# Interleaving feed-forward and attention in finer parts, and moving unused matmuls within the head

## The chip, the cores and the metric

The kernel runs on one core of a Trainium2 chip. The metric is the device time of one execution in microseconds (us). The profile's span, from the first to the last instruction, is about 1.8 us shorter than that time, and I use spans and parts of spans where I compare traces. Engines: PE is TensorE (matmuls), PEld its weight loads, DVE is VectorE, ACT is ScalarE, POOL is GpSimd, SP is SyncE, which issues DMAs. Matmuls write to PSUM; "evacuation" is ACT or DVE copying a finished PSUM tile to SBUF.

Each execution also has a mean granted clock of TensorE, as a share of full speed.

## The reference

Sinkhorn attention, then a bilinear feed-forward. There are 4 batches, 8 heads, 768 tokens and head size 64; tokens form 8 blocks of 96.

```python
for _ in range(5):                       # sort_net: [4, 8, 8, 8]
    P = exp(P - max(P)); P /= sum(P, -1); P /= sum(P, -2)
k_sorted = einsum('bhij,bhjcd->bhicd', P, k_blocks)      # "mix" of k
v_sorted = einsum('bhij,bhjcd->bhicd', P, v_blocks)      # "mix" of v
attn = softmax(scale * q_block @ k_sorted_block.T)       # 96 x 96 in each block
x = attn @ v_sorted                      # -> [3072, 512]
out = (x @ w_a) * (x @ w_b) @ w_out      # 512 -> 1536 -> 512
```

## The kernel before

All matmuls are bf16. PE's order is fixed by hand: in each stretch the feed-forward of one batch is the stream, and the attention of the next batch is cut into units that are placed between its steps. The first batch is split in two halves. The head (0 to 22 us) is the softmax iterations and the first half batch's attention, with nothing to interleave, so the author added unused matmuls (`keep_busy`).

```python
def keep_busy(ps, n, cols=512):          # unused matmuls on zeros
    for _ in range(n):
        nc.tensor.matmul(ps[:, 0:cols], lhsT=warm[:, 0:P], rhs=warm[:, 0:cols], ...)
...
keep_busy(heat[:, 0], (0, 4, 3, 2, 4)[it])          # in softmax iteration `it`
...
half_mix(0, 0, "k", "act", fill=2, cols=256)        # fill: keep_busy ahead of the mix
half_mix(0, 2, "k", "act", fill=1)
half_mix(0, 3, "k", "act", fill=1)
half_mix(0, 3, "v", "act", fill=1)
```

The attention of one head pair g, as units of the full stretches. The unit `o` multiplies the exponentials of the scores by v; a transpose of its result (the "x turn") then feeds the feed-forward. The array is used in three shapes: mixes and q turns as two column halves (128x64), scores as two row halves (64x128), and everything else whole (128x128, or 96 rows of it).

```python
def c_(g):                               # one unit
    if g < 2 * HP: turn_q(g)             # transposes of q, 128x64
    stage_mix(g, "k", ("act",))          # 12 matmuls, 128x64
    stage_mix(g, "v", ("dve", "act"))    # 12 matmuls, 128x64
    ...
def s_(g):                               # one unit
    stage_scores(g)                      # two halves of 8 matmuls, 64x128
    if g < 2 * HP: turn_v(g)             # transposes of v, whole array
def o_(g):                               # one unit
    stage_o(g)                           # two halves of 8 matmuls, whole array
    to_xT(g); ...
for n in range(HP + 1):
    if n < HP: us += [c_(g0 + n), s_(g0 + n)]       # (as closures)
    if n > 0:  us += [o_(g0 + n - 1)]
```

The feed-forward steps between which units go: `ffn_ab` makes one 128x384 tile of both first products (4 + 4 matmuls of 384 columns, tiles `pf`), `ffn_out` one block of the second product (12 matmuls of 512 columns, tile `po`). In the second half of batch 0, five first products were started early.

The softmax here doesn't subtract the row's maximum and nothing guards it: scores larger than these inputs give would overflow.

Of the kernel before, what the change touches and what calls it, by code (L numbers as in the profile page):

```python
# [9 lines left out]
FP32 = mybir.dt.float32  # L10
BF16 = mybir.dt.bfloat16
AF = mybir.ActivationFunctionType
# [10 lines left out]
def kernel(  # L23
# [11 lines left out]
    nc = tc.nc  # L35
    P = 128
    B, H, S, D = q.shape
    NB = sort_net.shape[-1]
# [126 lines left out]
    def keep_busy(ps, n, cols=512):  # L165
        for _ in range(n):
            nc.tensor.matmul(ps[:, 0:cols], lhsT=warm[:, 0:P], rhs=warm[:, 0:cols],  # L167
                             start=True, stop=True)
# [134 lines left out]
            nc.sync.dma_start_transpose(out=vss[g % NBUF][:, :, V0:V0 + P],  # L303
                                        in_=to.rearrange("p i t -> p (i t)"))

    def stage_scores(g):
        kT, qT, eT = kTs[g % NBUF], st[g, "qT"], eTs[g % NBUF]
        for hf in range(2):
            sc = psA.tile([P, 2, 512], FP32, tag="A", name="sc")
            for i in range(NBH):  # L310
                for e in range(2):
                    blk = hf * NBH + i
                    nc.tensor.matmul(  # L313
                        sc[:, e, i * BLK:(i + 1) * BLK],
                        lhsT=kT[e * D:(e + 1) * D, blk * BLK:blk * BLK + P],
                        rhs=qT[e * D:(e + 1) * D, :, blk * CG:(blk + 1) * CG],
                        start=True, stop=True)
            nc.scalar.activation(out=eT[:, hf, :, 0:HB], in_=sc[0:BLK, :, 0:HB],  # L318
                                 func=AF.Exp, scale=float(scale))

    def stage_o(g):
        xp = att.tile([BLK, NB, 2, D], BF16, tag="xp", name="xp")
        for hf in range(2):
            one_o(eTs[g % NBUF], hf, vss[g % NBUF], hf * NBH, xp, NB)
        st[g, "xp"] = xp

    def to_xT(g):
        xT, xp = xT_of(g // HP), st[g, "xp"]
# [17 lines left out]
    def hT_of(b):  # L346
        if b not in hTs:
            hTs[b] = ffp.tile([P, KO, S], BF16, tag="hT", name="hT")
        return hTs[b]

    def ffn_ab(b, m, t, begun=()):
        hT = hT_of(b)
        ab = []
        for n, w_sb in enumerate((w_a_sb, w_b_sb)):
            if n < len(begun):
                pf, k0 = begun[n], KA - 1
            else:
                pf, k0 = psF.tile([P, 512], FP32, tag="F", name="pf"), 0
            ab_mms(pf, w_sb, b, m, t, range(k0, KA))
            ab.append(pf)  # L360
            if n == 0:
                a_sb = ffp.tile([P, HW], BF16, tag="a_sb", name="a_sb", bufs=4)
                nc.scalar.copy(out=a_sb, in_=pf[:, 0:HW])  # L363
        nc.vector.tensor_mul(out=hT[:, m, t * HW:(t + 1) * HW], in0=a_sb,  # L364
                             in1=ab[1][:, 0:HW])

    def ffn_last(b, c):
        hT = hTs[b]
# [9 lines left out]

    def ffn_out(b, c):
        if b == B - 1 and c == NCH - 1:  # L380
            ffn_last(b, c)
            return
        hT = hTs[b]
        po = psF.tile([P, DMODEL], FP32, tag="F", name="po")
        for m in range(KO):
            nc.tensor.matmul(po, lhsT=hT[:, m, c * P:(c + 1) * P], rhs=w_out_sb[:, m, :],  # L386
                             start=(m == 0), stop=(m == KO - 1))
        o_sb = ffp.tile([P, DMODEL], FP32, tag="o_sb", name="o_sb", bufs=3)
        copy("act" if c % 2 == 0 else "dve", o_sb, po)
        if b == 0:  # L390
            h, u = divmod(c, 3)
            for c2 in range(2):
                nc.sync.dma_start(
                    out=_ap(out, (h * PH * NCH + 2 * u + c2) * DMODEL,
                            [[NCH * DMODEL, PH], [1, DMODEL]]),
                    in_=o_sb[c2 * PH:(c2 + 1) * PH])
        else:
            rows = out[b * S:(b + 1) * S, :].rearrange("(p c) n -> c p n", c=NCH)
            nc.sync.dma_start(out=rows[c], in_=o_sb)


    with tc.manual_schedule(engines={ET.PE, ET.Pool, ET.SP}):
        with tc.manual_schedule(engines={ET.Activation, ET.DVE}):
# [7 lines left out]
            for it in range(5):  # L411
# [14 lines left out]
                if it > 0:  # L426
                    nc.tensor.matmul(heat[0:NB, 1, 0:NB], lhsT=rsum, rhs=rsum,
                                     start=True, stop=True)
                    keep_busy(heat[:, 0], (0, 4, 3, 2, 4)[it])
                nc.vector.tensor_mul(out=p_nat, in0=p_nat,  # L430
                                     in1=_ap(rsum, 0, [[NB, BH], [1, NB], [0, NB]]))
                nc.vector.reduce_sum(out=csum, in_=p_nat.transpose([0, 2, 1]), axis=AX.X)
# [29 lines left out]
            load_ab(2)  # L462
            load_ab(3)

            half_mix(0, 0, "k", "act", fill=2, cols=256)
            half_mix(0, 0, "v", "dve")
            to_columns(1)
            half_mix(0, 1, "k", "act")
# [2 lines left out]
            half_scores(0, 0)  # L471
            half_v(0, 0)
            half_mix(0, 1, "v", "dve")
            half_mix(0, 2, "k", "act", fill=1)
            half_o(0, 0)
            half_scores(0, 1)
            half_v(0, 1)
            half_mix(0, 2, "v", "act")
            half_mix(0, 3, "k", "act", fill=1)
            half_x(0, 0, "dve")  # L480
            half_o(0, 1)
            half_scores(0, 2)
            half_v(0, 2)
            half_mix(0, 3, "v", "act", fill=1)
            half_x(0, 1, "dve")
            half_o(0, 2)
            half_scores(0, 3)
# [27 lines left out]


        def units_half():
            Q = [lambda hp=hp: half_q(1, hp, "dve") for hp in range(HP)]

            def M(hp):  # L520
                half_mix(1, hp, "k", "act")
                half_mix(1, hp, "v", "act")

            def R(hp):
                half_scores(1, hp)
                half_v(1, hp)

            us = [Q[0], lambda: M(0), Q[1]]
            for hp in range(HP):
                if hp + 1 < HP:  # L530
                    us.append(lambda hp=hp: M(hp + 1))
                us.append(lambda hp=hp: R(hp))
                if hp + 2 < HP:
                    us.append(Q[hp + 2])
                if hp > 0:
                    us.append(lambda hp=hp: half_x(1, hp - 1, "dve"))
                us.append(lambda hp=hp: half_o(1, hp))
            us.append(lambda: half_x(1, HP - 1, "dve"))
            return us

        def units_full(b):
            g0, us = b * HP, []

            def c_(g):
                if g < 2 * HP:
                    turn_q(g)
                stage_mix(g, "k", ("act",))
                stage_mix(g, "v", ("dve", "act"))
                if 2 * HP <= g < 3 * HP:
                    nc.gpsimd.tensor_copy(out=gate, in_=kTs[g % NBUF][0:1, 0:1])  # L550
                    load_pair(3, g % HP)

            def s_(g):
                stage_scores(g)
                if g < 2 * HP:
                    turn_v(g)

            def o_(g):
                stage_o(g)
                to_xT(g)  # L560
                if g < 2 * HP:
                    stage_q(g + HP)
                if 3 * HP <= g + 3 < B * HP:
                    pair_q(g + 3)
                    stage_q(g + 3)

            for n in range(HP + 1):
                if n < HP:
                    us.append(lambda g=g0 + n: c_(g))
                    us.append(lambda g=g0 + n: s_(g))  # L570
                if n > 0:
                    us.append(lambda g=g0 + n - 1: o_(g))
            return us

        def interleave(steps, units, spare, slow=0):
            n, done = len(steps), 0
            for s, step in enumerate(steps):
                step()
                want = s + 1 if s < slow else -(-(s + 1) * len(units) // (n - spare))
                while done < min(want, len(units)):  # L580
                    units[done]()
                    done += 1

        def paced(ab, po, units, spare):
            steps = [(1, f) for f in ab] + [(2, f) for f in po]
            total = sum(t for t, f in steps) - 2 * spare
            now = done = 0
            for t, step in steps:
                step()
                now += t  # L590
                while done < len(units) and done * total < now * len(units):
                    units[done]()
                    done += 1

        steps = [lambda: ffn_ab(0, 0, 0, begun[0:2]), lambda: ffn_ab(0, 1, 0, begun[2:4]),
                 lambda: ffn_ab(0, 2, 0, begun[4:5])]
        steps += [lambda m=m: ffn_ab(0, m, 0) for m in range(3, KO)]
        interleave(steps, units_half(), 1, 3)

        for b in range(B):  # L600
            ab = [lambda m=m, t=t, b=b: ffn_ab(b, m, t)
                  for m in range(KO) for t in range(2) if b > 0 or t == 1]
            po = [lambda c=c, b=b: ffn_out(b, c) for c in range(NCH)]
            paced(ab, po, units_full(b + 1) if b + 1 < B else [], 3 if b == 0 else 2)


# [28 lines left out]
```

## Time and profile before

| | before |
|---|---|
| time, median of 6 runs | 250.89 us (250.7 to 251.3) |
| span of the profile | 249.2 us |
| head, to the first feed-forward matmul | 21.70 us |
| second half of batch 0, to 48.45 | 26.75 us |
| batch 1's attention, to 90.06 | 41.61 us |
| batch 2's attention, to 144.59 | 54.53 us |
| batch 3's attention, to 199.11 | 54.52 us |
| feed-forward of batch 3 alone | 50.10 us |

From the page of the kernel before: the span, PE's busy time, the granted clock in 40 slices (in tenths), and the chain of waits by engine.

```profile
span 249.2 us, 5660 instructions
...
PE 239.0 (96%) x2330; PEld 139.8 (56%) x2342; DVE 112.8 (45%) x267; ACT 102.8 (41%) x203; POOL 59.4 (24%) x83
...
PEclk9999999999999999999999999999999999999999
...
PE 90%; DMA 2%; POOL 2%; DVE 2%; issue 1%; ACT 1%; POOLq 0%; DVEq 0%
```

PE bounds the kernel. But "96% busy" is no measure of headroom: a matmul's recorded duration overlaps the next one's (a `pf` matmul of 384 columns is recorded with 327 ns, and the next one starts 162 ns after it). So I read PE by the gap from one matmul's start to the next one's: 162 ns at 384 columns and 216 ns at 512, when nothing breaks the stream.

The timeline of PE in the kernel before, in the stretch of batch 2 (start, duration, engine, line, operation; xN matmuls in the row):

```profile
90.71 0.81 PE L343 MATMUL pf<-xT,w_b_sb 128*128 128x384 bf16 x4
91.45 0.53 PE L292 MATMUL mix<-s_all,k 128*64 128x128 bf16 x12
91.81 0.50 PE L292 MATMUL mix<-s_all,v 128*64 128x128 bf16 x12
92.25 0.82 PE L343 MATMUL pf<-xT,w_a_sb 128*128 128x384 bf16 x4
...
94.21 0.81 PE L343 MATMUL pf<-xT,w_b_sb 128*128 128x384 bf16 x4
94.95 0.52 PE L313 MATMUL sc<-qTf,kT 64*128 64x96 bf16 x16
95.40 0.82 PE L343 MATMUL pf<-xT,w_a_sb 128*128 128x384 bf16 x4
```

Four `pf` matmuls take 4 x 162 ns = 0.65 us, as from one `pf` row to the next elsewhere; from 90.71 to the mix at 91.45 it is 0.74. From k's mix to v's mix (no change of shape) it is 0.36 us, from v's mix to the next `pf` 0.44. That is the price of changing the array's shape: some 0.09 us going in, some 0.1 coming out.

And a real wait, in the stretch of batch 1 (the last bracket is the engine's idle time and what ended it):

```profile
73.71 0.50 PE L292 MATMUL mix<-s_all,v 128*64 128x128 bf16 x12
...
74.26 0.56 DVE L163 CAST vT<-mix 128x384 bf16<-128x384 f32 x1
74.84 0.34 PE L313 MATMUL sc<-qT,kT 64*128 64x96 bf16 x8 [0.62 <-DVE vT L163]
74.85 0.48 ACT L161 CAST vT<-mix 128x384 bf16<-128x384 f32 x1
...
75.38 0.35 PE L313 MATMUL sc<-qT,kT 64*128 64x96 bf16 x8 [0.20 <-ACT vT L161]
```

Here q's turn, both mixes and the scores follow one another without a feed-forward step between, and the scores wait for the mixes' evacuation.

### The profile page before, as it was taken

How to read it: one execution, taken by the hardware profiler on the slowest of the kernel's cores; microseconds unless marked ns; L12 is line 12 of the kernel's file. 1: busy time of each engine (PE TensorE's matmuls, PEld its weight loads, DVE VectorE, ACT ScalarE, POOL GpSimd, SP SyncE). 2: the span in 40 equal slices, each digit the busy share in tenths (PEclk: the TensorE clock that was granted, in tenths of full speed). 3: DMA queues.
4: the chain of work that ended last, by engine and by line, in shares of the span. 5: the costliest groups of instructions: out<-in, count | busy, mean ns of one | idle time of the engine just before them, and what ended most of it. 6: DMA issues, size and time to landing. Idle time of an engine off the chain costs nothing.

```text
span 249.2 us, 5660 instructions
## 1 busy us (share of the span) xinstructions
PE 239.0 (96%) x2330; PEld 139.8 (56%) x2342; DVE 112.8 (45%) x267; ACT 102.8 (41%) x203; POOL 59.4 (24%) x83
## 2 busy tenths in 40 slices
PE   7789899999999999999999999999999999999994
PEld 2366566666655455666655456666645456655443
DVE  6774546655654323464633334363616144444110
ACT  3365656366633035636343146645440033333001
POOL 8975579439300002305061000000000000000000
PEclk9999999999999999999999999999999999999999
DMA  6999999999832869646584831232134310000122
GB/s 81 198 199 197 197 202 198 207 202 202 98 63 54 168 141 158 95 78 90 85 130 128 201 102 31 45 63 45 33 82 116 121 42 3 0 0 4 42 114 97
DMA packets 49162, 26.85 MB, mean 108 GB/s; under 512 B 25968, under 2 KB 46192, under 8 KB 49136
## 3 DMA queue, kind: packets, MB, share of 16 engines
q0 software_dynamic: 20944, 14.16, 39.0%
q1 hardware_dynamic: 28048, 12.27, 21.3%
q8 instruction: 18, 0.29, 0.5%
q10 hardware_dynamic: 144, 0.07, 0.1%
q14 instruction: 8, 0.07, 0.1%
HBM read 28.32 MB, written 6.29 MB: 139 GB/s over the span
## 4 chain that ended last, share of the span: by engine, by line
PE 90%; DMA 2%; POOL 2%; DVE 2%; issue 1%; ACT 1%; POOLq 0%; DVEq 0%
PE pf L343 50%; PE po L386 24%; PE mix L292 4%; PE o_ps L242 3%; DMA v<-in_v_dram 2%; PE sc L313 2%; PE mixh L192 1%; PE po L373 1%; PE vs_ps L282 1%; PE sc L207 1%; PE vs_ps L219 1%; PE q_ps L271 1%; PE xt_ps L233 1%; DVE hT L364 1%; DVE xph L248 1%
## 5 line engine op out<-in xcount | busy, mean ns | idle before, releaser
L364 DVE TENSOR_TENSOR hT<-a_sb,pf 128x384 bf16<-128x384 bf16 x95 | 52.5, 553 | 73.1 <-PE pf L343 49.2
L343 PE MATMUL pf<-xT,w_a_sb 128*128 128x384 bf16 x380 | 77.9, 327 | 0.0
L343 PE MATMUL pf<-xT,w_b_sb 128*128 128x384 bf16 x380 | 77.4, 326 | 0.0
L363 ACT CAST a_sb<-pf 128x384 bf16<-128x384 f32 x95 | 45.5, 479 | 63.9 <-PE pf L343 42.6
L386 PE MATMUL po<-w_out_sb,hT 128*128 128x512 bf16 x265 | 60.5, 379 | 0.6
L343 PEld LDWEIGHTS <-w_b_sb 128*128 128x128 bf16 x384 | 37.5, 98 | 24.9 <-issue 0.3
L343 PEld LDWEIGHTS <-w_a_sb 128*128 128x128 bf16 x384 | 34.9, 98 | 22.1
L386 PEld LDWEIGHTS <-hT 128*128 128x128 bf16 x276 | 26.4, 98 | 30.2
L161 ACT COPY o_sb<-po 128x512 f32<-128x512 f32 (+1 forms) x13 | 7.5, 577 | 50.5 <-PE po L386 49.1
L163 DVE COPY o_sb<-po 128x512 f32<-128x512 f32 (+1 forms) x12 | 7.9, 658 | 42.5 <-PE po L386 37.0
L318 ACT ACTIVATE eT<-sc 96x768 bf16<-96x768 f32 x24 | 18.1, 803 | 3.2 <-PE sc L313 3.2
L248 DVE TENSOR_TENSOR xp<-o_ps,rec 96x512 bf16<-96x512 f32 x24 | 15.7, 683 | 0.2
L161 ACT CAST kT<-mix 128x384 bf16<-128x384 f32 x24 | 10.3, 482 | 7.9 <-PE mix L292 7.9
L94 POOL DMA_DIRECT2D k<-in_k_dram x16 | 11.6, 728 | 6.1 <-PE pf L343 3.6
L94 POOL DMA_DIRECT2D v<-in_v_dram x16 | 11.6, 726 | 4.8 <-PE pf L343 3.1
L242 PEld LDWEIGHTS <-eT 96*128 96x128 bf16 x256 | 10.3, 97 | 3.3 <-ACT eT L211 0.7
L550 POOL COPY gate<-kT 1x1 bf16<-1x1 bf16 x4 | 0.7, 178 | 47.3 <-ACT kT L161 47.3
L242 PE MATMUL o_ps<-vs,eT 96*128 96x65 bf16 x256 | 11.2, 193 | 0.6 <-ACT eT L211 0.6
L94 POOL DMA_DIRECT2D q<-in_q_dram x12 | 8.7, 724 | 3.2 <-DMA w_out_sb<-in_moe_w_out_dram 1.6
L257 POOL COPY qc<-q 128x768 bf16<-128x768 bf16 x8 | 6.6, 842 | 8.1 <-DMA q<-in_q_dram 8.1
L167 PE MATMUL heat<-warm 128*128 128x512 bf16 x20 | 6.9, 484 | 1.4 <-DVE warm L77 1.3
L211 ACT ACTIVATE eT<-sc 96x768 bf16<-96x768 f32 x8 | 6.5, 808 | 3.3 <-PE sc L207 3.3
(81 smaller groups left out, 162.3 us busy)
## 6 DMA issues: line engine op xcount, KB each, us to landing
out_dram<-o_sb SPq DMA_DIRECT2D x17, 256.0 KB, 2.0
k<-in_k_dram POOLq DMA_DIRECT2D x16, 192.0 KB, 6.5
v<-in_v_dram POOLq DMA_DIRECT2D x16, 192.0 KB, 6.4
q<-in_q_dram POOLq DMA_DIRECT2D x12, 192.0 KB, 7.0
w_a_sb<-in_moe_w_a_dram POOLq DMA_DIRECT2D x6, 256.0 KB, 10.6
w_b_sb<-in_moe_w_b_dram POOLq DMA_DIRECT2D x6, 256.0 KB, 10.7
w_out_sb<-in_moe_w_out_dram POOLq DMA_DIRECT2D x3, 512.0 KB, 10.0
out_dram<-o_sb SPq DMA_DIRECT2D x12, 128.0 KB, 2.4
```

What stands on the lines that cost most here:

```text
L94: nc.gpsimd.dma_start(out=to, in_=_ap(t, base, [[W, P], [S * D, 2], [1, W]]))
L161: nc.scalar.copy(out=out, in_=in_)
L163: nc.vector.tensor_copy(out=out, in_=in_)
L167: nc.tensor.matmul(ps[:, 0:cols], lhsT=warm[:, 0:P], rhs=warm[:, 0:cols], start=True, stop=True)
L242: nc.tensor.matmul(o_ps[:, e, i * (D + 1):(i + 1) * (D + 1)], lhsT=eT[:, hf, e, i * BLK:i * BLK + P], rhs=vs[0:BLK, i0 + i, V0 - 1 + e * ( ...
L248: nc.vector.tensor_tensor(out=_ap(xp, i0 * 2 * D, [[nxp * 2 * D, BLK], [D, 2], [2 * D, NBH], [1, D]]), in0=_ap(o_ps, 1, [[1024, BLK], [511 ...
L292: nc.tensor.matmul(mix[e * D:(e + 1) * D, c // 3, c % 3 * P:(c % 3 + 1) * P], lhsT=src2[:, e, c * D:(c + 1) * D], rhs=s_all[:, 2 * g + e], ...
L318: nc.scalar.activation(out=eT[:, hf, :, 0:HB], in_=sc[0:BLK, :, 0:HB], func=AF.Exp, scale=float(scale))
L343: nc.tensor.matmul(pf[:, 0:HW], lhsT=w_sb[:, kc, m * P:(m + 1) * P], rhs=x_cols(b, kc, t), start=(kc == 0), stop=(kc == KA - 1))
L363: nc.scalar.copy(out=a_sb, in_=pf[:, 0:HW])
L364: nc.vector.tensor_mul(out=hT[:, m, t * HW:(t + 1) * HW], in0=a_sb, in1=ab[1][:, 0:HW])
L386: nc.tensor.matmul(po, lhsT=hT[:, m, c * P:(c + 1) * P], rhs=w_out_sb[:, m, :], start=(m == 0), stop=(m == KO - 1))
```

## The change

Its intent: place attention in smaller units between smaller feed-forward steps, so that PE never reaches a unit whose evacuation isn't done; and, now that the head is taken to be dense enough, drop the three unused matmuls between its mixes, with one more in each of two softmax iterations and two wider ones ahead of the first mix. In columns this is a move and not a cut: 3 x 512 go, 2 x 512 + 2 x 256 come, so both kernels have 12800 unused columns in all. What becomes thinner is the part of the head between its mixes; that is what "thin head" means below.

```diff
-                    keep_busy(heat[:, 0], (0, 4, 3, 2, 4)[it])
+                    keep_busy(heat[:, 0], (0, 4, 3, 3, 5)[it])
-            half_mix(0, 0, "k", "act", fill=2, cols=256)
+            half_mix(0, 0, "k", "act", fill=2)
-            half_mix(0, 2, "k", "act", fill=1)
+            half_mix(0, 2, "k", "act")
-            half_mix(0, 3, "k", "act", fill=1)
+            half_mix(0, 3, "k", "act")
-            half_mix(0, 3, "v", "act", fill=1)
+            half_mix(0, 3, "v", "act")
 ... units_half: second half of batch 0
-            (Q, M = k and v mix, R = scores and v turn, O, X as units)
+            order = ("Q0 k0 v0 Q1 S0 k1 V0 v1 O0 Q2 S1 k2 V1 X0 v2 O1 Q3 S2 k3 V2 X1 v3 O2 "
+                     "S3 V3 X2 O3 X3").split()
 ... units_full: the three full stretches
-                    us.append(lambda g=g0 + n: c_(g))
-                    us.append(lambda g=g0 + n: s_(g))
-                    us.append(lambda g=g0 + n - 1: o_(g))
+                us += [lambda g=g: k_(g)] * new
+                us += [lambda g=g: turn_q(g)] * (new and b == 1)
+                us += [lambda g=g: stage_mix(g, "v", ("dve", "act"))] * new
+                us += [lambda g=g: stage_scores(g, 0)] * new
+                us += [lambda g=g: o_(g - 1, 0)] * old
+                us += [lambda g=g: stage_scores(g, 1)] * new
+                us += [lambda g=g: o_(g - 1, 1)] * old
+                us += [lambda g=g: turn_v(g)] * (new and b == 1)
 ... ffn_ab now returns two steps (w_a, w_b: 4 matmuls each), ffn_out two of 6 matmuls;
 ... paced() places units by matmuls done
```

More of the change, by code (lines that the diff above doesn't have):

```diff
@@ L304, in stage_mix, with stage_scores, stage_o @@
                                         in_=to.rearrange("p i t -> p (i t)"))
-    def stage_scores(g):
+    def stage_scores(g, hf):
         kT, qT, eT = kTs[g % NBUF], st[g, "qT"], eTs[g % NBUF]
-        for hf in range(2):
-            sc = psA.tile([P, 2, 512], FP32, tag="A", name="sc")
-            for i in range(NBH):
-                for e in range(2):
-                    blk = hf * NBH + i
-                    nc.tensor.matmul(
-                        sc[:, e, i * BLK:(i + 1) * BLK],
-                        lhsT=kT[e * D:(e + 1) * D, blk * BLK:blk * BLK + P],
-                        rhs=qT[e * D:(e + 1) * D, :, blk * CG:(blk + 1) * CG],
-                        start=True, stop=True)
-            nc.scalar.activation(out=eT[:, hf, :, 0:HB], in_=sc[0:BLK, :, 0:HB],
-                                 func=AF.Exp, scale=float(scale))
-    def stage_o(g):
-        xp = att.tile([BLK, NB, 2, D], BF16, tag="xp", name="xp")
-        for hf in range(2):
-            one_o(eTs[g % NBUF], hf, vss[g % NBUF], hf * NBH, xp, NB)
-        st[g, "xp"] = xp
+        sc = psA.tile([P, 2, 512], FP32, tag="A", name="sc")
+        for i in range(NBH):
+            for e in range(2):
+                blk = hf * NBH + i
+                nc.tensor.matmul(
+                    sc[:, e, i * BLK:(i + 1) * BLK],
+                    lhsT=kT[e * D:(e + 1) * D, blk * BLK:blk * BLK + P],
+                    rhs=qT[e * D:(e + 1) * D, :, blk * CG:(blk + 1) * CG],
+                    start=True, stop=True)
+        nc.scalar.activation(out=eT[:, hf, :, 0:HB], in_=sc[0:BLK, :, 0:HB],
+                             func=AF.Exp, scale=float(scale))
+    def stage_o(g, hf):
+        if hf == 0:
+            st[g, "xp"] = att.tile([BLK, NB, 2, D], BF16, tag="xp", name="xp")
+        one_o(eTs[g % NBUF], hf, vss[g % NBUF], hf * NBH, st[g, "xp"], NB)
     def to_xT(g):
@@ L351, in ffn_ab, with part @@
     def ffn_ab(b, m, t, begun=()):
-        hT = hT_of(b)
-        ab = []
-        for n, w_sb in enumerate((w_a_sb, w_b_sb)):
+        held = {}
+        def part(n, w_sb):
             if n < len(begun):
@@ L359, in ffn_ab @@
             ab_mms(pf, w_sb, b, m, t, range(k0, KA))
-            ab.append(pf)
             if n == 0:
-                a_sb = ffp.tile([P, HW], BF16, tag="a_sb", name="a_sb", bufs=4)
-                nc.scalar.copy(out=a_sb, in_=pf[:, 0:HW])
-        nc.vector.tensor_mul(out=hT[:, m, t * HW:(t + 1) * HW], in0=a_sb,
-                             in1=ab[1][:, 0:HW])
+                held["a"] = ffp.tile([P, HW], BF16, tag="a_sb", name="a_sb", bufs=4)
+                nc.scalar.copy(out=held["a"], in_=pf[:, 0:HW])
+            else:
+                nc.vector.tensor_mul(out=hT_of(b)[:, m, t * HW:(t + 1) * HW],
+                                     in0=held["a"], in1=pf[:, 0:HW])
+        return [(1 if n < len(begun) else KA, lambda n=n, w_sb=w_sb: part(n, w_sb))
+                for n, w_sb in enumerate((w_a_sb, w_b_sb))]
     def ffn_last(b, c):
@@ L380, in ffn_out, with part, store @@
         if b == B - 1 and c == NCH - 1:
-            ffn_last(b, c)
-            return
-        hT = hTs[b]
-        po = psF.tile([P, DMODEL], FP32, tag="F", name="po")
-        for m in range(KO):
-            nc.tensor.matmul(po, lhsT=hT[:, m, c * P:(c + 1) * P], rhs=w_out_sb[:, m, :],
-                             start=(m == 0), stop=(m == KO - 1))
+            return [(2 * KA * 2, lambda: ffn_last(b, c))]
+        held = {}
+        def part(n):
+            if n == 0:
+                held["po"] = psF.tile([P, DMODEL], FP32, tag="F", name="po")
+            for m in range(n * KO // 2, (n + 1) * KO // 2):
+                nc.tensor.matmul(held["po"], lhsT=hTs[b][:, m, c * P:(c + 1) * P],
+                                 rhs=w_out_sb[:, m, :], start=(m == 0), stop=(m == KO - 1))
+            if n == 1:
+                store(b, c, held["po"])
+        return [(2 * KA, lambda n=n: part(n)) for n in range(2)]
+    def store(b, c, po):
         o_sb = ffp.tile([P, DMODEL], FP32, tag="o_sb", name="o_sb", bufs=3)
@@ L517, in units_half, with one, o_ @@
         def units_half():
-            Q = [lambda hp=hp: half_q(1, hp, "dve") for hp in range(HP)]
-            def M(hp):
-                half_mix(1, hp, "k", "act")
-                half_mix(1, hp, "v", "act")
-            def R(hp):
-                half_scores(1, hp)
-                half_v(1, hp)
-            us = [Q[0], lambda: M(0), Q[1]]
-            for hp in range(HP):
-                if hp + 1 < HP:
-                    us.append(lambda hp=hp: M(hp + 1))
-                us.append(lambda hp=hp: R(hp))
-                if hp + 2 < HP:
-                    us.append(Q[hp + 2])
-                if hp > 0:
-                    us.append(lambda hp=hp: half_x(1, hp - 1, "dve"))
-                us.append(lambda hp=hp: half_o(1, hp))
-            us.append(lambda: half_x(1, HP - 1, "dve"))
-            return us
+            def one(what, hp):
+                if what == "Q":
+                    half_q(1, hp, "dve")
+                elif what in "kv":
+                    half_mix(1, hp, what, "act")
+                elif what == "S":
+                    half_scores(1, hp)
+                elif what == "V":
+                    half_v(1, hp)
+                elif what == "O":
+                    half_o(1, hp)
+                else:
+                    half_x(1, hp, "dve")
+            order = ("Q0 k0 v0 Q1 S0 k1 V0 v1 O0 Q2 S1 k2 V1 X0 v2 O1 Q3 S2 k3 V2 X1 v3 O2 "
+                     "S3 V3 X2 O3 X3").split()
+            return [lambda u=u: one(u[0], int(u[1])) for u in order]
         def units_full(b):
             g0, us = b * HP, []
-            def c_(g):
-                if g < 2 * HP:
-                    turn_q(g)
-                stage_mix(g, "k", ("act",))
-                stage_mix(g, "v", ("dve", "act"))
-                if 2 * HP <= g < 3 * HP:
-                    nc.gpsimd.tensor_copy(out=gate, in_=kTs[g % NBUF][0:1, 0:1])
-                    load_pair(3, g % HP)
-            def s_(g):
-                stage_scores(g)
-                if g < 2 * HP:
-                    turn_v(g)
-            def o_(g):
-                stage_o(g)
+            def o_(g, hf):
+                stage_o(g, hf)
+                if hf == 0:
+                    return
                 to_xT(g)
@@ L565, in o_, with k_, paced @@
                     stage_q(g + 3)
-            for n in range(HP + 1):
-                if n < HP:
-                    us.append(lambda g=g0 + n: c_(g))
-                    us.append(lambda g=g0 + n: s_(g))
-                if n > 0:
-                    us.append(lambda g=g0 + n - 1: o_(g))
-            return us
-        def interleave(steps, units, spare, slow=0):
-            n, done = len(steps), 0
-            for s, step in enumerate(steps):
-                step()
-                want = s + 1 if s < slow else -(-(s + 1) * len(units) // (n - spare))
-                while done < min(want, len(units)):
-                    units[done]()
-                    done += 1
-        def paced(ab, po, units, spare):
-            steps = [(1, f) for f in ab] + [(2, f) for f in po]
-            total = sum(t for t, f in steps) - 2 * spare
+            def k_(g):
+                stage_mix(g, "k", ("act",))
+                if 2 * HP <= g < 3 * HP:
+                    nc.gpsimd.tensor_copy(out=gate, in_=kTs[g % NBUF][0:1, 0:1])
+                    load_pair(3, g % HP)
+            for n in range(HP + 1):
+                g, new, old = g0 + n, n < HP, n > 0
+                us += [lambda g=g: k_(g)] * new
[6 more added lines that the diff above has]
+                us += [lambda g=g: turn_v(g)] * (new and b == 1)
+            return us
+        def paced(steps, units, spare):
+            total = sum(t for t, f in steps) - spare
             now = done = 0
@@ L593, in paced @@
                     done += 1
-        steps = [lambda: ffn_ab(0, 0, 0, begun[0:2]), lambda: ffn_ab(0, 1, 0, begun[2:4]),
-                 lambda: ffn_ab(0, 2, 0, begun[4:5])]
-        steps += [lambda m=m: ffn_ab(0, m, 0) for m in range(3, KO)]
-        interleave(steps, units_half(), 1, 3)
+        steps = []
+        for m in range(KO):
+            steps += ffn_ab(0, m, 0, begun[2 * m:2 * m + 2])
+        paced(steps, units_half(), 2 * KA)
         for b in range(B):
-            ab = [lambda m=m, t=t, b=b: ffn_ab(b, m, t)
-                  for m in range(KO) for t in range(2) if b > 0 or t == 1]
-            po = [lambda c=c, b=b: ffn_out(b, c) for c in range(NCH)]
-            paced(ab, po, units_full(b + 1) if b + 1 < B else [], 3 if b == 0 else 2)
+            steps = []
+            for m in range(KO):
+                for t in range(2) if b > 0 else (1,):
+                    steps += ffn_ab(b, m, t)
+            for c in range(NCH):
+                steps += ffn_out(b, c)
+            paced(steps, units_full(b + 1) if b + 1 < B else [], 12 * KA if b == 0 else 8 * KA)
 _INS = ['q', 'k', 'v', 'sort_net', 'moe_w_a', 'moe_w_b', 'moe_w_out']
```

## The prediction

> **What bounds the kernel.** TensorE. The page gives PE 96% busy, DVE 45%, ACT 41%; the chain that ended last is 90% PE; the granted clock is 1.0 from 5 us on. The timeline of PE, read as start-to-start gaps, shows steady 162 ns (384 columns) and 216 ns (512 columns), so the time is the sum of those gaps plus what breaks the stream.
>
> **What breaks the stream.** (1) Changes between differently shaped array uses (128x128; 128x64 mixes and q-turns; 64x128 scores). A gap of 162 ns before a mix becomes 256, before scores 258; the last mix matmul is followed after 152 ns instead of 53, the last score after 135 instead of 40. So each change costs about 95 ns, a visit of mix or scores about 190. Entering 128x128 work (o, v-turns) adds nothing. [...] (2) Real waits: about 0.5 and 0.8 us near 26 and 30 us, 0.3 at 45 (o to x of the last pair), 1.4 at 74–75.4 (scores waiting for the v mix's evacuation), 0.8 at 17.5 for nothing shown.
>
> **What the change does.** By the built order on PE:
> - The head loses three unused 512-column matmuls between mixes (0.32 us each with their two mode changes). Two are added in the softmax iterations, where PE waits anyway; two grow from 256 to 512 columns (+0.05 us). ACT does about 1.77 us per head pair there (0.48+0.81+0.48), nearly PE's 1.9, so I expect 0.4 us of 0.96.
> - Second half of batch 0: mode changes 24 to 29 (+0.5 us). The waits at 26 and 30 shrink (−1.0), but the last o now has only 4 matmuls (0.65 us) before its x turn, and needs reciprocal and multiply (0.2+0.69): +0.5. Net 0.
> - The three interleaved stretches after it: mode changes 15 to 38, 16 to 32, 16 to 32, as k, v and the score halves no longer sit together. 55 more at 95 ns: +5.3 us.
> - The 1.4 us wait at 74 goes, as k, v and scores are now six matmuls (1.3 us) apart. But the last v-turn of that stretch is now followed directly by the o product that needs its evacuation (0.69 plus latency): +0.9.
>
> All of this is on the critical path, as PE is. The last 50 us don't change. Sum: −0.4 + 0 + 5.3 − 1.4 + 0.9 = +4.4, less some 0.4 for small waits I cannot name: 255.0 us. Range 253.3 to 256.8. Even if every wait after 22 us (about 4 us) vanished, the mode changes would eat it. Chances: faster by over 2% 0.02, within 2% 0.76, slower by over 2% 0.22.
>
> **What would show it.** Each of the two 54 us stretches (one batch's start to the next's) longer by about 1.5 us, the stretch from 46 to 90 longer by about 1.7; gaps at the mode changes unchanged near 95 ns but 56 more of them; no 0.8 us gap of PE at 74; a new gap of about 0.9 us between the last v-turn and o; head shorter by 0.3 to 0.6 us; clock 1.0 throughout.
>
> **What would make it wrong.** The clock dropping in the thinner head [...]; [...] new waits for PSUM buffers or for xT, whose last transposes have 6.5 us, not 7.7, to land.

A note on reading it. Its sum is +4.4 us, less 0.4 for waits without a name: +4.0, or 255.0 us. Its figures for changes of shape are gaps in the trace of the kernel before. "Adds nothing" rests on gaps too: 162 or 163 ns from the last `pf` matmul to the first of o, and 215 or 216 from the last `po`, as between two of `pf` or two of `po` (for v turns, in the changed kernel, 161 to 163 and 216). What a drop of the clock costs was measured later: 1.2 to 1.4 us in e2, 2.3 to 2.7 in e9.

## The result

| | before | changed |
|---|---|---|
| time, median of 6 runs | 250.89 us (250.7 to 251.3) | 259.25 us (257.37 to 260.25) |
| span of the profile | 249.2 us | 255.8 us, clock 0.998 |
| head | 21.70 | 21.63 |
| second half of batch 0 | 26.75 | 26.85 |
| batch 1's attention | 41.61 | 44.70 |
| batch 2's attention | 54.53 | 56.29 |
| batch 3's attention | 54.52 | 56.28 |
| feed-forward of batch 3 alone | 50.10 | 50.10 |

The ratio is 1.032 with a 95% interval of 1.0274 to 1.0367. Ratios here are the mean time of one kernel's fast runs over that of the other's fast runs of the same rounds, so they are not quite the ratio of the medians quoted. The change is slower, and slower than I had said. The six executions also scatter: at clock 0.998 they took 257.37 and 257.62 us, at 0.993 258.65, at 0.985 to 0.987 259.85 to 260.25. (In the profile at 0.998 the clock falls only 1.2 us before the end, so that one lost nothing in the head. All are marked "fast": none is over 1.5% above the kernel's fastest run.)

So there are two losses. One is in every execution: the two profiles, both at nearly full clock, differ by 255.8 - 249.2 = 6.6 us. The other comes with a lower clock in four of six.

From the page of the changed kernel:

```profile
span 255.8 us, 5648 instructions
...
PE 245.8 (96%) x2329; PEld 137.7 (54%) x2341; DVE 115.6 (45%) x267; ACT 104.2 (41%) x203; POOL 59.3 (23%) x83
...
PEclk9999999999999999999999999999999999999999
...
PE 91%; DMA 2%; POOL 2%; DVE 1%; issue 1%; ACT 0%; POOLq 0%; DVEq 0%
```

The share is the same 96%. Where the time went is seen by stretch. First the kernel before, then the changed one: the stretch, its length, then busy time and number of instructions of each engine; PE, with its matmuls, is the first:

```profile
48.45:90.06 41.61, 40.63 (x462) 24.61 (x465) 20.71 (x42) 17.75 (x34) 11.79 (x13) 1.00 0.82 136
90.06:144.59 54.53, 54.37 (x487) 31.41 (x489) 23.31 (x47) 23.79 (x47) 12.65 (x20) 1.00 0.67 123
144.59:199.11 54.52, 54.36 (x486) 31.42 (x488) 23.39 (x47) 23.79 (x47) 0.00 (x0) 1.00 0.28 68
```

```profile
48.48:93.18 44.70, 43.76 (x466) 24.26 (x469) 21.48 (x43) 18.69 (x35) 12.08 (x13) 1.00 0.74 130
93.18:149.47 56.29, 56.13 (x487) 30.97 (x489) 24.08 (x47) 24.27 (x47) 12.61 (x20) 1.00 0.68 117
149.47:205.75 56.28, 56.12 (x486) 30.98 (x488) 24.09 (x47) 24.35 (x47) 0.00 (x0) 1.00 0.27 66
```

In batches 2 and 3 PE runs the same 487 and 486 recorded matmuls at the same clock, is "busy" all the time in both, and takes 1.76 us longer in each. (The stretch of batch 1 has four more feed-forward matmuls in the change, 0.65 us, which lay in the stretch before it: set right, that is +2.44 us for batch 1 and +0.75 for the second half of batch 0.)

PE's timeline of the changed kernel in the stretch of batch 2:

```profile
93.18 0.81 PE L341 MATMUL pf<-xT,w_a_sb 128*128 128x384 bf16 x4
93.92 0.53 PE L292 MATMUL mix<-s_all,k 128*64 128x128 bf16 x12
94.38 0.82 PE L341 MATMUL pf<-xT,w_b_sb 128*128 128x384 bf16 x4
95.04 0.81 PE L341 MATMUL pf<-xT,w_a_sb 128*128 128x384 bf16 x4
95.79 0.53 PE L292 MATMUL mix<-s_all,v 128*64 128x128 bf16 x12
96.25 0.82 PE L341 MATMUL pf<-xT,w_b_sb 128*128 128x384 bf16 x4
```

k's and v's mixes are now two visits. Each takes 0.46 us to the next `pf` (93.92 to 94.38, 95.79 to 96.25), and the `pf` row ahead of each takes 0.74 or 0.75 instead of 0.65. In the kernel before both mixes together took 0.80 (91.45 to 92.25) and one such row.

In the stretch of batch 1 the wait at 74 us is gone, and a new one has come (all engines; weight loads left out):

```profile
82.22 0.61 PE L282 MATMUL vs_ps<-ident,vT 128*128 128x128 bf16 x8
...
82.86 0.69 DVE L283 COPY vs<-vs_ps 96x1024 bf16<-96x1024 bf16 x1 [0.82 <-PE vs_ps L282]
83.61 0.42 PE L242 MATMUL o_ps<-vs,eT 96*128 96x65 bf16 x8 [0.78 <-DVE vs L283]
```

In the second half of batch 0 a wait at 26 us has grown: the second of the two products that share the PSUM tile `two` waits until DVE has read the first. In the kernel before, two mixes ran in between:

```profile
25.22 0.33 PE L343 MATMUL two<-xT,w_b_sb 128*128 128x384 bf16 x1
...
25.93 0.55 DVE L364 TENSOR_TENSOR hT<-a_sb,two 128x384 bf16<-128x384 bf16 x1
...
26.54 0.32 PE L343 MATMUL two<-xT,w_a_sb 128*128 128x384 bf16 x1 [0.36 <-DVE hT L364]
```

In the changed kernel:

```profile
25.55 0.34 PE L341 MATMUL two<-xT,w_b_sb 128*128 128x384 bf16 x1
...
26.00 0.56 DVE L362 TENSOR_TENSOR hT<-a_sb,two 128x384 bf16<-128x384 bf16 x1 [0.18 <-PE two L341]
...
26.60 0.32 PE L341 MATMUL two<-xT,w_a_sb 128*128 128x384 bf16 x1 [0.71 <-DVE hT L362]
```

### The profile page after: what moved, and what is told of

The parts are those of the page before. It is cut to its first block, busy times and chain, and to the rows that moved or that the text cites. A ratio compares the mean times of both kernels' runs of the same rounds, so it can differ in the third digit from the quotient of the medians.

```text
span 255.8 us, 5648 instructions
## 1 busy us (share of the span) xinstructions
PE 245.8 (96%) x2329; PEld 137.7 (54%) x2341; DVE 115.6 (45%) x267; ACT 104.2 (41%) x203; POOL 59.3 (23%) x83
## 2 busy tenths in 40 slices
DMA packets 49162, 26.85 MB, mean 105 GB/s; under 512 B 25968, under 2 KB 46192, under 8 KB 49136
## 4 chain that ended last, share of the span: by engine, by line
PE 91%; DMA 2%; POOL 2%; DVE 1%; issue 1%; ACT 0%; POOLq 0%; DVEq 0%
PE pf L341 50%; PE po L389 23%; PE mix L292 4%; PE o_ps L242 4%; PE sc L312 3%; DMA v<-in_v_dram 2%; PE mixh L192 1%; PE po L374 1%; PE xt_ps L233 1%; PE sc L207 1%; PE vs_ps L282 1%; PE q_ps L271 1%; PE vs_ps L219 1%; PE two L341 1%; DVE xph L248 1%
## 5 line engine op out<-in xcount | busy, mean ns | idle before, releaser
L389 PE MATMUL po<-w_out_sb,hT 128*128 128x512 bf16 x265 | 62.5, 379 | 0.6
L341 PEld LDWEIGHTS <-w_b_sb 128*128 128x128 bf16 x384 | 34.1, 97 | 22.5 <-issue 0.9
L389 PEld LDWEIGHTS <-hT 128*128 128x128 bf16 x276 | 25.6, 98 | 28.3
L317 ACT ACTIVATE eT<-sc 96x768 bf16<-96x768 f32 x24 | 19.4, 809 | 9.8 <-PE sc L312 9.8
L248 DVE TENSOR_TENSOR xp<-o_ps,rec 96x512 bf16<-96x512 f32 x24 | 16.5, 686 | 0.8
L242 PEld LDWEIGHTS <-eT 96*128 96x128 bf16 x256 | 11.7, 98 | 5.7 <-DVE vs L283 1.0
L246 DVE RECIPROCAL rec<-o_ps 96x8 f32<-96x8 f32 x32 | 6.5, 203 | 17.2 <-PE o_ps L242 17.1
L242 PE MATMUL o_ps<-vs,eT 96*128 96x65 bf16 x256 | 13.2, 193 | 1.0 <-DVE vs L283 0.8
L161 ACT CAST vT<-mix 128x384 bf16<-128x384 f32 x12 | 5.8, 480 | 12.0 <-DVE vT L163 12.0
L312 PEld LDWEIGHTS <-kT 64*128 64x128 bf16 x192 | 4.8, 94 | 8.2 <-issue 7.2
```

Source lines behind the costliest of these rows:

```text
L161: nc.scalar.copy(out=out, in_=in_)
L242: nc.tensor.matmul(o_ps[:, e, i * (D + 1):(i + 1) * (D + 1)], lhsT=eT[:, hf, e, i * BLK:i * BLK + P], rhs=vs[0:BLK, i0 + i, V0 - 1 + e * ( ...
L248: nc.vector.tensor_tensor(out=_ap(xp, i0 * 2 * D, [[nxp * 2 * D, BLK], [D, 2], [2 * D, NBH], [1, D]]), in0=_ap(o_ps, 1, [[1024, BLK], [511 ...
L312: nc.tensor.matmul(sc[:, e, i * BLK:(i + 1) * BLK], lhsT=kT[e * D:(e + 1) * D, blk * BLK:blk * BLK + P], rhs=qT[e * D:(e + 1) * D, :, blk ...
L317: nc.scalar.activation(out=eT[:, hf, :, 0:HB], in_=sc[0:BLK, :, 0:HB], func=AF.Exp, scale=float(scale))
L341: nc.tensor.matmul(pf[:, 0:HW], lhsT=w_sb[:, kc, m * P:(m + 1) * P], rhs=x_cols(b, kc, t), start=(kc == 0), stop=(kc == KA - 1))
```

## The experiments

Theory A has two parts: the extra changes of the array's shape cost about 0.1 us each in every execution, and the thinner head lets the clock fall in most executions. The rivals: B, it is the finer interleave itself that lowers the clock; C, it is the interruptions of the feed-forward stream (or its halved steps, with PSUM tiles held longer) that cost, whatever shape the visitor has. All runs gave correct results. I call a clock under 0.995 low.

### e1: the head's unused matmuls put back in the changed kernel

```diff
-keep_busy(heat[:, 0], (0, 4, 3, 3, 5)[it])
+keep_busy(heat[:, 0], (0, 4, 3, 2, 4)[it])
 (and fill=2, cols=256 / fill=1 / fill=1 / fill=1 as before)
```

> The changed kernel, with only the unused matmuls of the first half batch and of the softmax iterations put back as they were before. Theory A ([...] the extra mode changes cost about 6 us in every execution): mean granted clock 0.997 or more in every execution, all executions within 1 us of 257.4 us, span of the profile 255 to 256.5. Rival B (the finer interleave[...]): executions at clock 0.985 to 0.993 and 258.5 to 260 us as often as in the changed kernel (5 of 6).

Measured: 257.71 to 258.01 us in four executions, all at clock 0.998 or more, span 256.2 us. The scatter is gone and the 6.6 us stay (medians of 257.84 and 251.23 us in the same rounds). The verdict by the 2% rule is "unclear" (ratio 1.0249, interval 1.0187 to 1.0311), because one of the seven executions of the kernel before took 253.73 us at clock 0.985; the other six span 251.0 to 251.3. Rival B falls.

### e2: the thin head alone, in the kernel before

```diff
-keep_busy(heat[:, 0], (0, 4, 3, 2, 4)[it])
+keep_busy(heat[:, 0], (0, 4, 3, 3, 5)[it])
 (and the fills of the change)
```

> The kernel before, with only the unused matmuls changed as in the change (three taken out between mixes, two wider, two more in the softmax iterations). Theory A: some executions at clock 0.985 to 0.993, those 1.2 to 2.6 us longer than the kernel before; an execution at clock 1.0 equals the kernel before within 0.4 us (250.5 to 251.1). Rival B: clock 1.0 in all executions, 250.5 to 251.1.

Measured: 250.91 and 250.92 us at clock 1.0, 252.14 and 252.28 us at 0.992 and 0.991; the kernel before in the same rounds 251.23 us in the median. (The two at a low clock are 1.2 to 1.4 us above the other two, but only 0.9 to 1.05 above that median, a little under the 1.2 expected.) So the thin head by itself brings the low clock, without any finer interleave. What it gains where the clock holds is about 0.1 us: spans of 249.1 us against 249.2 to 249.5 for the kernel before where it kept its clock. Of the 0.4 us that I had expected from it hardly anything is left.

### e3: attention regrouped, everything else as changed

```diff
 (shortened)
-us += k_, turn_q, v mix, scores 0, o 0 (old), scores 1, o 1 (old), turn_v    # eight units
+us += [turn_q + k_ + v mix], [scores 0 + scores 1 + turn_v], [o 0 + o 1 (old)]  # three units
```

> The changed kernel, with finer feed-forward steps, head and second half batch kept, but in the three full stretches k, q turn and v, the two score halves, and the two o halves each back in one unit. Mode changes on PE by the built order: 16, 16, 16 there instead of 38, 32, 32. Theory A (each mode change costs about 0.1 us): batches 2 and 3 take 54.5 us each again instead of 56.3, and the span is 5 to 6 us below the changed kernel's at equal clock, so 250 to 251 at clock 1.0. Rival C (the halved feed-forward steps and their longer-held PSUM tiles cost the time): batches 2 and 3 stay at 56 us or more.

Measured: batches 2 and 3 take 54.52 us each again, with the halved feed-forward steps kept:

```profile
90.13:144.65 54.52, 54.52 (x490) 31.42 (x489) 23.58 (x47) 24.01 (x47) 12.65 (x20) 1.00 0.67 122
144.65:199.17 54.52, 54.52 (x490) 31.41 (x489) 23.58 (x47) 24.09 (x47) 0.00 (x0) 1.00 0.29 68
```

The profile's span is 249.3 us at clock 0.998, 6.5 us less than the changed kernel's (5 to 6 were expected). Grouping is what cost, not the halved steps. The median of the four executions is 252.19 us, as three of them had a clock of 0.992 or 0.993 (this kernel keeps the thin head).

The stretch of batch 1 is 41.65 us, with the four more `pf` matmuls in it: the halved steps on their own save 0.61 us there, as q, k and v on one side and the scores on the other now have six `po` matmuls between them.

### e4: the changed kernel again

No edit.

> The changed kernel once more, on the same chip, to catch a profile at a lower clock. Theory A: executions fall into groups by mean clock, 0.998, 0.993 and 0.987, [...] about 1.2 us of time for each; a profile at less than 0.998 shows the half clock between about 10 and 22 us from the start, in the first half batch. Rival B: it shows the half clock after 45 us, where the finer stretches lie.

Measured: 258.4, 259.18 and 259.37 us at 0.993, 0.993 and 0.992, 259.98 at 0.986; none at 0.998. This time the profile caught it: the clock is granted at 6.15 us, falls to half at 19.80, 13.65 us later, and is back at 23.21. e2's profile shows the same: granted at 7.17, half from 20.83, 13.65 us later. So it is in the first half batch and just after, not in the finer stretches. The times don't fall into such clean groups as I had expected: the two at 0.993 differ by 0.8 us, and the runs don't show why.

### e5: the halved steps and two moves in the kernel before

Own unused matmuls, own grouping, own second half of batch 0 but for two moves:

```diff
 (ffn_ab, ffn_out and paced as in the change; units_full as in e3; head and units_half as before)
+(the last matmul of the started product (m=2, w_a) now runs right after that of (m=1, w_b),
+ ahead of the read of (m=1, w_b): both are halves of the tile `two`)
-us = [..., scores+v turn of pair 0, Q2, O0, mixes of pair 2, ...]
+us = [..., scores+v turn of pair 0, Q2, mixes of pair 2, O0, ...]
```

> The kernel before, with its own unused matmuls, its own second half batch but for two moves, and its own grouping of k, v, scores and o; kept from the change are only the halved feed-forward steps in the three full stretches. The two moves: the started product that shares a PSUM tile with its neighbour is finished before the neighbour is read (takes away the 0.43 us wait near 26 us), and the first o of the second half waits for one more mix (takes away some of the 0.66 us wait for the exponential at 30 us). Expected: batches 2 and 3 54.5 us each as before; the wait for v's evacuation near 74 us (0.71+0.4 us) gone, so the stretch to 90 us about 0.6 shorter; together 1.2 to 1.8 us below the kernel before, span 247.4 to 248.0, 249.2 to 249.8 us, clock 1.0 in nearly all executions.

Measured: 249.23 us median of five (248.96 to 249.52), clock 0.998 or more in all; ratio to the kernel before 0.9929, interval 0.9915 to 0.9942; span 247.5 us. This version beats both kernels. (The gain of 0.7% is small, but clear of the noise.) Its second half of batch 0 is 24.94 us, and with the four `pf` matmuls set right 1.16 us shorter than before. That goes with the two moves, which were not run one by one: in the trace the wait at 26 us is gone and the one for the exponential fell from 0.68 to 0.19 us. Batch 1 gives the 0.6 us of e3; batches 2 and 3 take 54.52 us each. Of the gain only these 0.6 us come from the change, without what it cost; the moves are new.

### e6 and e7: one split that changes shape, and one that doesn't

Both start from e5 without its two moves.

```diff
 e6, batches 2 and 3 only
-us.append(lambda g=g: s_(g))                 # both score halves
+us.append(lambda g=g: stage_scores(g, 0))
+us.append(lambda g=g: stage_scores(g, 1))
 e7, batches 2 and 3 only
-us.append(lambda g=g: oo_(g))                # both o halves
+us.append(lambda g=g: o_(g, 0))
+us.append(lambda g=g: o_(g, 1))
```

> Feed-forward steps halved, grouping of before, but in batches 2 and 3 the two score halves are apart: 8 more mode changes in each stretch (24 instead of 16), nothing else added. Theory A (each mode change costs 105 to 115 ns: 95 at the change and the rest in the first matmuls after it): both stretches 54.53 + 0.84 to 0.92 = 55.4 us. Rival C (an interruption of the feed-forward stream costs, whatever its shape): the same here, but also in the next run.

> The same, but instead of the scores the two o halves are apart in batches 2 and 3: as many more interruptions (4 per stretch), no mode change more (16). Theory A: both stretches stay at 54.5 us (within 0.1). Rival C: 55.4 us.

Measured, the two stretches of e6 and then of e7 (the second number is the length):

```profile
89.18:144.55 55.37, 55.21 (x487) 31.19 (x489) 23.96 (x47) 24.35 (x47) 12.65 (x20) 1.00 0.70 116
144.55:199.92 55.37, 55.21 (x486) 31.20 (x488) 23.95 (x47) 24.42 (x47) 0.00 (x0) 1.00 0.30 71
```

```profile
88.91:143.45 54.54, 54.43 (x488) 31.41 (x488) 24.36 (x47) 24.00 (x47) 12.64 (x20) 1.00 0.65 122
143.45:197.98 54.53, 54.42 (x487) 31.40 (x488) 24.36 (x47) 24.07 (x47) 0.00 (x0) 1.00 0.28 68
```

Four more visits of scores add 0.84 us to each stretch: 105 ns for each of the eight changes of shape. Four more visits of o, which leave the array whole, add 0.01 us. Rival C falls: an interruption costs nothing, the change of shape does. Times of these single looks were 251.81 and 249.88 us; a single execution's state is unknown, but their clocks were 1.0 and 0.999.

### e8: the last v turn one unit earlier

In the changed kernel with the head of e1:

```diff
+us += [lambda g=g: turn_v(g)] * (new and b == 1)
 us += [lambda g=g: o_(g - 1, 1)] * old
-us += [lambda g=g: turn_v(g)] * (new and b == 1)
```

> The changed kernel with before's unused matmuls (as e1), and each v turn of batch 1 one unit earlier, ahead of the second o half of the pair before it, so that the last v turn no longer stands right ahead of the o product that reads its evacuation. Expected: the 0.95 us gap of PE near 83 us gone, the stretch from the first full mix to batch 2's start 43.8 us instead of 44.71, everything else as in e1. If it stays at 44.7, another wait takes its place and the gap was not what the order cost.

Measured: the stretch is 43.75 us against e1's 44.71, the other full stretches are the same to 0.01 us, and the time is 256.78 us (a single look, clock 1.0). PE's timeline of e8 at that place:

```profile
80.75 0.62 PE L282 MATMUL vs_ps<-ident,vT 128*128 128x128 bf16 x8
81.21 1.46 PE L389 MATMUL po<-w_out_sb,hT 128*128 128x512 bf16 x6
82.50 0.66 PE L242 MATMUL o_ps<-vs,eT 96*128 96x65 bf16 x16
```

Six `po` matmuls now stand between the turn and the product that needs its evacuation, and nothing waits. The wait was worth 0.96 us.

### e9 and e10: one unused matmul put back, at two places

```diff
 e9
-half_mix(0, 3, "v", "act")
+half_mix(0, 3, "v", "act", fill=1)
 e10
-half_mix(0, 2, "k", "act")
+half_mix(0, 2, "k", "act", fill=1)
```

From the starts of the matmuls I had worked out which share of a stretch the array streams columns, at 0.42 ns a column (216 ns for 512). Stretches are counted from where the clock was granted (6.15 us in e4, 7.17 in e2, the two that had shown the fall so far), and 3.41 us is the length of e4's stretch at half clock.

> The changed kernel with one of the three unused matmuls put back: the last, ahead of v's mix of the fourth head pair, which ran at 18.9 us in the kernel before. [...] the clock fell at the end of the fourth stretch of 3.41 us, that is at 19.8 and 20.8 us, and the stretch before it was the emptiest of all runs (the array streams 0.40 and 0.42 of it; 0.43 and more where it held). One matmul of 216 ns adds 0.06 there. Theory A in this sharper form: the mean clock is 0.997 or more in at least 4 of 5 timed executions, 257.2 to 258.0 us. Rival (any unused matmul does[...]): the same here and in the next run.

> The changed kernel with the first of the three put back instead, ahead of k's mix of the third head pair, which ran at 14.4 us in the kernel before, ahead of that stretch. Theory A in its sharper form: it doesn't help: 0.985 to 0.994 in most executions, 258.4 to 260.3 us, as in the changed kernel (8 of 10 so far). Rival: 0.997 or more in most executions, as in the run before.

Measured: e9 had a low clock in 2 of 6 executions (0.985 twice, 260.1 us), its profile, at 1.0, took 257.45 us; e10 in 3 of 6 (0.986, 0.993, 0.987; 258.97 to 260.47 us). Both expectations missed: e9 needed four good executions of its five timed ones and had three; e10 should have been bad in most and was in two of its five timed ones and in the profile. The two don't differ by enough to say that the place matters. e10's profile is the clearest picture of the event, though. Windows of 3.41 us of e10, counted from where the clock was granted (PE busy is the first number after the length; the share of the clock stands third from the end):

```profile
12.36:15.77 3.41, 3.41 (x95) 2.42 (x93) 2.47 (x7) 2.09 (x4) 2.82 (x5) 1.00 1.40 197
15.77:19.19 3.42, 2.30 (x60) 1.69 (x54) 2.39 (x6) 1.76 (x5) 2.70 (x4) 1.00 1.38 201
19.19:22.60 3.41, 3.36 (x52) 2.64 (x50) 2.09 (x5) 2.31 (x4) 1.65 (x3) 0.50 1.46 200
22.60:26.01 3.41, 3.41 (x17) 1.74 (x15) 0.89 (x2) 0.13 (x2) 1.35 (x3) 0.50 1.44 193
26.01:29.40 3.39, 2.67 (x36) 1.37 (x35) 1.44 (x3) 1.80 (x4) 2.08 (x3) 1.00 1.45 196
```

After a window in which PE is busy for 2.30 of 3.42 us, two follow at half the clock, and in the second of them only 17 matmuls run. But that busy share does not decide it. The same window of e1, whose clock held, is no busier, and the longest gap from the end of one recorded matmul to the start of the next in it is 1.13 us, as in e10 (1.12):

```profile
16.93:20.34 3.41, 2.28 (x51) 1.70 (x51) 1.76 (x5) 1.74 (x3) 1.69 (x2) 1.00 1.39 196
```

The span of e10's execution is 258.5 us, 2.7 us over the first profile of the changed kernel. All three profiles that caught the event lose the clock 13.65 us (four windows) after it was granted. In these three the array streamed 0.41, 0.42 and 0.40 of the window just before (e10, e4, e2; matmuls side by side in the array counted once); in the nine profiles that kept the clock 0.43 to 0.54 of the same window (0.43 in e1, 0.47 in the kernel before). So the three lie below the nine, but three against nine, of a number that I made and with so thin a gap (0.42 to 0.43), is a hint and not a proof.

Over all executions whose clock is listed, the thin head without any unused matmul between the mixes (the changed kernel, e2, e3, e4) had a low clock in 13 of 18; with one put back (e9, e10) in 5 of 12; with all of them (e1, e5, e6, e7, e8) in none of 12; and the kernel before, in the rounds of these experiments, in 2 of 27. These runs lie on three chips (e1 to e4 on one, e5 to e8 on another, e9 and e10 on a third; that of the changed kernel's first six is not on record), so the groups are not quite like for like; on the first chip alone it is 9 of 12 without, none of 4 with all, and 1 of 7 in the kernel before. And no run separates the three matmuls taken out from the two added and two widened earlier in the head: e1 and e2 switch all of them together.

## Why the prediction was wrong

The main mechanism was right: PE's changes of shape. Two things carry the miss. The clock, which I had named among the things that could upset the sum but had given no share in it, did fall: about 1.8 us of the 4.3 that were missing. And the gains I had subtracted (0.4 in the head, 1.0 at 26 and 30 us, 1.4 at 74, 0.4 unnamed) came to about 1.3 us instead of 3.2, another 1.9. The cost of a change of shape, 105 ns or more instead of 95, is only some 0.5 us of it. Point by point, at full clock first:

| term | predicted | measured |
|---|---|---|
| head | -0.4 | -0.07 (traces); about -0.1 (e2) |
| second half of batch 0 | 0 | +0.75 |
| 55 more changes of shape | +5.3 | 55 x 0.105 = +5.8; +1.76 of it measured in each of batches 2 and 3 |
| wait at 74 us | -1.4 | about -0.9 (not measured alone: what is left of batch 1's +2.44) |
| v turn ahead of o | +0.9 | +0.96 (e8) |
| small waits, unnamed | -0.4 | nothing |
| sum | +4.0 | 255.8 - 249.2 = +6.6 |

- **"So each change costs about 95 ns": mis-sized.** I took the gap at the change itself. The first pair of matmuls after it is slow too: in the trace the first gap within a mix is 77 ns after a change and 53 without, and the first gap of `pf` after a visit 173 instead of 162. e6 measures the whole for scores: 105 ns for one change. For the four mixes and four scores that each of batches 2 and 3 visits once more, 16 changes at 110 ns make the 1.76 us; take e6's 0.84 off, and the mixes' eight changes come to about 115 ns each (by difference; no run split the mixes alone).
- **"The waits at 26 and 30 shrink (-1.0)": failed.** The wait for the exponential at 30 us went (0.68 us less). The one at 26 us grew from about 0.54 us (0.43 ahead of the second product, 0.11 between the two mixes) to 0.89 us, because its cause is the shared tile `two`: the finer order leaves it shared, and takes away the two mixes that had stood between its two products. "+0.5" for the last o and its x turn was +0.27, with 0.16 more ahead of that o. So the waits gave nothing, and six more changes of shape (counted from the traces) cost 0.6.
- **"I expect 0.4 us of 0.96" in the head: failed.** It is 0.1. I have not tested what took up the rest; the changed kernel's trace has longer waits of PE elsewhere in the head, 1.15 us at 17.3 us, for nothing that the profile shows (before: 0.96 at 17.5), and 0.55 at 12.7, where PE waits for POOL's `p_rep` (before: 0.22).
- **The wait at 74 us**: I called it 1.4 us from start to start; PE was held for 0.7 and 0.4 of that.
- **"Clock 1.0 throughout": failed.** Four of six executions lost it, by their mean clock for one window or two (an estimate from e4's 3.41 us at half clock: one costs 3.41 x 0.5 / 257 = 0.0066 of the mean). The changed kernel's ten executions of both submissions give 257.4 and 257.6 us where the clock held, and 259.5 us on average in the other eight. The low clock is the rest of the measured 8.4 us: 6.6 in every execution and about 1.8 in the median one.
- **What held**: no faster outcome; the new gap between v turn and o, of the size given; no wait at 74 us; the last 50 us unchanged (50.10 in both); gaps at the changes as before (256 ns into a mix, 258 into scores, 152 and 135 out, in both), and 55 more of them in the three interleaved stretches, counted from the traces. The stretches themselves grew by more than I had said: by 1.76 us instead of 1.5 in batches 2 and 3, by 2.44 instead of 1.7 in batch 1.

Even at full clock the time, 257.4 us, lies above the range (256.8): the range was built around waits that would go, and together with the head they gave less than half of what I had counted on.

Of the clock, the traces show this. In the kernel before it is granted at 5.13 us, and until then PE had run only unused matmuls and two of 32x8; the unused ones, of 512 columns, start 427 ns apart before it and 216 after it. In the others quoted here the first grant lies between 5.51 us (the changed kernel) and 7.17 (e2). The stretches at half clock in the head lasted 3.41 us in e4 and 6.82 in e10.

## What to carry to other kernels

When PE is the bound, count the changes of array shape in the built order before cutting work finer: here each cost 105 ns or a little more, and the 61 added after the head together some 6.4 us (an estimate at 105 ns), far more than the waits that the cutting removed, while cutting work of one shape cost nothing (0.01 us in e7). Keep visitors of one shape together, and put space between a producer and its consumer by halving the host stream's steps or by moving one unit. Matmuls that compute nothing may be holding the clock (it was low in 13 of 18 executions without those between the mixes, in none of 12 with all of them in e1 and e5 to e8); judge their removal by several executions with the clock of each, not by one trace.
